# Attention feeding two expert layers on one core: a weight split spread over eight periods, and the order of the value products

## The chip, the core and the metric

One NeuronCore of a Trainium2 chip runs the whole kernel in one launch. The time is the device time of one execution in microseconds (us). The engines have short names in the profile: PE (TensorE matmul), PEld (its weight loads), DVE (VectorE), ACT (ScalarE), POOL (GpSimd) and SP (SyncE, which here only issues transfers). Each engine runs its own instructions in order and waits on the others through semaphores.

## The reference

What is computed, cut to what matters:

```python
# q, k, v: (2, 12, 448, 64) f32; cap = 30
scores = cap * tanh((q @ k.T / 8) / cap)
attn = softmax(scores) with 1e-9 added to the sum
x = (attn @ v) as (896, 768)
h = max(x @ w1, x @ w2, x @ w3); x = h @ w_out
xn = x / rms(x) * g
out = (silu(xn @ w_gate) * (xn @ w_val)) @ w_out2
```

The weights arrive in float64. A weight is used as a high and a low part, and so is each activation, so that a matrix product costs three matmuls.

## The kernel before, in words

**Attention.** The 24 heads are taken as 12 pairs; a pair's two heads lie on the two halves of the partitions. The 448 keys of a pair are four blocks: three of 128 (c = 0, 1, 2) and a last one of 64 (c = 3, `KB`), whose two heads share one tile. `scores(i, c)` multiplies keys by queries into PSUM banks (line 210 for the blocks of 128, line 217 for the last), and ACT takes tanh from each bank into the tile of exponents (lines 212, 218). There are five such banks, so a product waits for the tanh of the fifth before it. `expo(i)` (line 222) is two ACT instructions that take exp of blocks 0 and 1, then of 2 and 3. The sums over keys are built block on block: `sum_01` (line 226) and `sum_3` (line 231, two instructions, one for each head) on POOL, `sum_2` (line 235) on DVE; `sum_all` (line 253) is a product with ones that adds over the partitions. `values` (line 247) accumulates exponents times values over the four blocks in one bank. `norm` (lines 257, 259: a reciprocal and a product) and `split_x` (lines 267, 268) on DVE finish a pair and cut it into its high and low parts.

A function `period(i)` writes out by hand what each engine does: for period i, norm of pair i - 2, `sum_2` of pair i - 1, `split_x` of pair i - 2, then scores of pair i, values and `sum_all` of pair i - 1, exp and block sums of pair i. Period 12 (`period(n)`) runs in `tail`, a hook inside the first matrix product of the second stage. The fp32 products come in pairs of records, one pair for the two heads side by side, so a block of 128 keys is four records.

**Weights.** They come in units of 128 x 768 float64. `load_unit` (lines 98, 99) makes two transfers on SP, `raw` and `mid`, each with two buffers. `split_unit` (lines 109 to 117) turns a unit into `whi` and `wlo` by eight instructions, then calls `load_next`, which starts the next load. For the first two units all eight run on DVE (`on_dve`). Unit 0 is split in period 0, unit 1 in period 1, unit 2 in the tail, the others by a planner that spreads them over the matrix products.

**Start.** Two products of zeros (`warm`, line 316) run on PE before the first scores. In the bounded case, which these inputs take, the order is that of `period`.

**After the attention** the matrix products follow (lines 277 and 531), about 447 us of the span.

Of the kernel before, what the change touches and what calls it, by code (L numbers as in the profile page):

```python
# [18 lines left out]
B, H, S, D = 2, 12, 448, 64  # L19
# [3 lines left out]
NC = S // CP  # L23
KB = S // P
# [16 lines left out]
def attn_moe_kernel(ctx, tc, bounded, qT, kT, v, cap, w123, wo, wgv, wo2, rms_g, out):  # L41
    nc = tc.nc
    pe, dve, act, pool, sp = nc.tensor, nc.vector, nc.scalar, nc.gpsimd, nc.sync
# [31 lines left out]
    def bank():  # L75
        return pp.tile([P, 512], F32, tag="b", name="bank", bufs=5)

    def bank_o():
        return pp.tile([P, 512], F32, tag="o", name="banko", bufs=2)

    def bank_s():
        return pp.tile([P, 512], F32, tag="s", name="banks", bufs=1)
# [16 lines left out]
        sp.dma_start(out=mid.rearrange("p a b -> p (a b)").bitcast(U16)[:, :4 * U - 2], in_=src.bitcast(U16)[:, 1:4 * U - 1])  # L99
        return raw[:, :, 1], mid[:, :, 0]  # L100

    def split_unit(words, on_dve):
        hi, lo = (gp.tile([P, U], F32R, tag="g", name=name, bufs=NG) for name in ("whi", "wlo"))
        f = wp.tile([P, U], U32, tag="f", name="f", bufs=2)
        d = wp.tile([P, U], U32, tag="d", name="d", bufs=1)
        high, mid = words
        ff = f.bitcast(F32)
        steps = [
            (lambda: dve.tensor_scalar(f, high, 0x7FFFFFFF, None, op0=ALU.bitwise_and)) if on_dve else
            (lambda: act.activation(ff, high.bitcast(F32), AF.Abs)),  # L110
            lambda: dve.tensor_scalar(ff, ff, W_MIN, W_MAX, op0=ALU.max, op1=ALU.min),  # L111
            lambda: dve.tensor_scalar(f, f, 3, 0x3FFFF000, op0=ALU.logical_shift_left, op1=ALU.bitwise_and),
            lambda: dve.scalar_tensor_tensor(f, high, 0xC0000000, f, op0=ALU.bitwise_and, op1=ALU.bitwise_or),  # L113
            lambda: (dve.tensor_copy if on_dve else act.copy)(hi, ff),  # L114
            lambda: dve.tensor_scalar(d, f, 0xFF800000, None, op0=ALU.bitwise_and),  # L115
            lambda: dve.tensor_scalar(mid, mid, 0x01FFFFFF, None, op0=ALU.bitwise_and),
            lambda: dve.scalar_tensor_tensor(lo, mid, 2.0 ** -36, d.bitcast(F32), op0=ALU.mult, op1=ALU.mult),  # L117
            load_next,
        ]
        for step in steps:  # L120
            step()
        return hi, lo

    unit_src = [w123[j, n] for j in range(KC) for n in range(3)]
# [4 lines left out]
    loaded, units = [], []  # L129
# [2 lines left out]
        if len(loaded) < len(unit_src):  # L132
            loaded.append(load_unit(unit_src[len(loaded)]))

    def split_next():
        i = len(units)
        units.append(split_unit(loaded[i], i < 2))
        loaded[i] = None

    with tc.manual_schedule():  # L140

        pairs = [(b, hp) for b in range(B) for hp in range(NP)]
        n = len(pairs)
        kq, vt, E, EX, Ssum, SB, PO, XS = {}, {}, {}, {}, {}, {}, {}, {}
        X = [None] * KC

        def load_pair(i):

            b, hp = pairs[i]
            k_, qv = tp.tile([P, S], F32, tag="k", name="k", bufs=3), big("qv")  # L150
            kq[i], vt[i] = (k_, qv[:, 0]), qv[:, 1]
            sp.dma_start(out=k_, in_=kT[b, hp])
            sp.dma_start(out=qv[:, 0], in_=qT[b, hp])

        def load_v(i):
            b, hp = pairs[i]
            sp.dma_start(out=vt[i], in_=v[b, hp])
# [36 lines left out]
        def blocks(i):  # L194

            t = quad("e01"), quad("e23")
            E[i] = [t[0][:, 0], t[0][:, 1], t[1][:, 0], t[1][:, 1, 0]]
            EX[i] = t[0].rearrange("p a j s -> p (a j s)"), t[1].rearrange("p a j s -> p (a j s)")[:, :3 * S]

        def scores(i, c):  # L200
            if i not in E:
                blocks(i)
            t = E[i][c]
            k_, q_ = kq[i]
            heads = [slice(j * D, (j + 1) * D) for j in range(2)]
            if c < KB:

                ps = [bank(), bank()]
                for j, rows in enumerate(heads):
                    pe.matmul(ps[j][:, :S], k_[rows, c * P:(c + 1) * P], q_[rows], start=True, stop=True)  # L210
                for j in range(2):
                    act.activation(t[:, j, :], ps[j][:, :S], AF.Tanh, scale=tsc)  # L212
            else:

                ps = bank()
                for rows in heads:
                    pe.matmul(ps[rows, :S], k_[rows, KB * P:], q_[rows], start=True, stop=True)  # L217
                act.activation(t, ps[:, :S], AF.Tanh, scale=tsc)

        def expo(i):  # L220
            for e in EX[i]:
                act.activation(e, e, AF.Exp, scale=cap_sb)  # L222
# [5 lines left out]
        def sum_3(i, eng):  # L228
            for j in range(2):
                rows = slice(j * KL, (j + 1) * KL)  # L230
                eng.tensor_add(Ssum[i][rows, j], Ssum[i][rows, j], E[i][KB][rows])

        def sum_2(i):

            dve.scalar_tensor_tensor(Ssum[i], E[i][2], guard, Ssum[i], op0=ALU.add, op1=ALU.add)  # L235

        def values(i, *blocks):
            for c in blocks:
                if c == 0:
                    PO[i] = bank_o()  # L240
                for j in range(2):
                    if c < KB:
                        w, e = vt[i][:, c * P + j * D:c * P + (j + 1) * D], E[i][c][:, j, :]
                    else:
                        rows = slice(j * KL, (j + 1) * KL)
                        w, e = vt[i][rows, KB * P:], E[i][c][rows]
                    pe.matmul(PO[i][64 * j:64 * j + 64, :S], w, e, start=(c == 0), stop=(c == KB))  # L247

        def sum_all(i):

            ps = SB[i] = bank_s()
            for j in range(2):
                pe.matmul(ps[64 * j:64 * j + 64, :S], ones, Ssum[i][:, j, :], start=True, stop=True)  # L253

        def norm(i):
            r = small("r")[:, :S]
            dve.reciprocal(r, SB.pop(i)[:, :S])  # L257
            xs = XS[i] = spare()
            dve.tensor_mul(xs, PO.pop(i)[:, :S], r)

        def split_x(i):
            b, hp = pairs[i]
            if b == 0:
                X[hp] = flat("x")
            hi, lo = (t[:, BATCH[b]] for t in X[hp])
            xs = XS.pop(i)
            dve.tensor_copy(hi, xs)
            dve.tensor_sub(lo, xs, hi.bitcast(F32))
# [43 lines left out]
        dve.memset(warm, 0.0)  # L312
        act.activation(tsc, warm[:, :1], AF.Exp)
        ps = bank()
        for _ in range(2):
            pe.matmul(ps[:, :S], warm[:, :P], warm, start=True, stop=True)
        load_next()
        load_pair(1)
# [12 lines left out]
        if bounded:  # L331

            guard = const.tile([P, 1], F32, name="guard")
            dve.tensor_scalar_mul(guard, cap_sb, -1.0)
            dve.tensor_tensor(guard, guard, cap_sb, op=ALU.min)
            act.activation(guard, guard, AF.Exp)
            dve.tensor_scalar_mul(guard, guard, 1e-9 / P)
            def period(i):

                if i + 2 < n:
                    load_pair(i + 2)
                    load_v(i + 2)
                if i >= 2:
                    norm(i - 2)
                if i == n:
                    sum_3(i - 1, dve)
                if i >= 1:
                    sum_2(i - 1)  # L350
                if i == 1:
                    split_next()
                if i >= 2:
                    split_x(i - 2)
                if i < n:
                    for c in range(NC):
                        scores(i, c)
                if i >= 1:
                    values(i - 1, 0, 1, 2)
                    sum_all(i - 1)  # L360
                    values(i - 1, 3)
                if i < n:
                    expo(i)
                    if i == 0:

                        split_next()
                        sum_01(i, dve)
                        sum_3(i, dve)
                    else:
                        sum_01(i, dve if i == n - 1 else pool)  # L370
                        if i < n - 1:
                            sum_3(i, pool)

            def tail():
                period(n)
                split_next()
                norm(n - 1)
                split_x(n - 1)

            for i in range(n):  # L380
                period(i)
        else:
            for i in range(n):
                if i + 2 < n:
                    load_pair(i + 2)
                    load_v(i + 2)
                attend(i)
            for _ in range(3):
                split_next()
# [153 lines left out]
        first = {}  # L543
# [5 lines left out]
        for u in range(len(unit_src) - 1, 2, -1):  # L549
            e = min(first[u] - AHEAD, nxt - SPACE)  # L550
# [56 lines left out]
```

## Time and profile before

| what | us |
|---|---|
| three timed runs | 554.73, 554.96, 556.86 |
| median of them | 554.96 |
| the profiled execution, its own time | 556.08 |
| its span, first to last instruction | 554.3 |
| PE busy in it | 539.7 (97%) |
| DVE busy | 415.0 (75%) |
| ACT busy | 240.6 (43%) |
| POOL busy | 59.2 (11%) |

A row of the time line tells the start, the duration, the engine, the line and operation, the tile written and the tiles read, and how many records were merged; in brackets stands the idle time of the engine ahead of it and what ended it. The busy shares are means over the span: the attention is its first fifth, and the rest is matrix products. The granted clock is a share of TensorE's full rate, so 0.50 is 1.2 GHz and 1.00 is 2.4 GHz.

### The profile page before, as it was taken

How to read it: one execution, taken by the hardware profiler on the slowest of the kernel's cores; microseconds unless marked ns; L12 is line 12 of the kernel's file. 1: busy time of each engine (PE TensorE's matmuls, PEld its weight loads, DVE VectorE, ACT ScalarE, POOL GpSimd, SP SyncE). 2: the span in 40 equal slices, each digit the busy share in tenths (PEclk: the TensorE clock that was granted, in tenths of full speed). 3: DMA queues.
4: the chain of work that ended last, by engine and by line, in shares of the span. 5: the costliest groups of instructions: out<-in, count | busy, mean ns of one | idle time of the engine just before them, and what ended most of it. 6: DMA issues, size and time to landing. Idle time of an engine off the chain costs nothing.

```text
span 554.3 us, 7037 instructions
## 1 busy us (share of the span) xinstructions
PE 539.7 (97%) x2682; PEld 438.3 (79%) x2682; DVE 415.0 (75%) x592; ACT 240.6 (43%) x347; POOL 59.2 (11%) x48
## 2 busy tenths in 40 slices
PE   7879999999999999999999999999999999999996
PEld 3223333479889999988998999988888999999996
DVE  4996777799998898686586888878777778836701
ACT  4858898714434333335454333333333333312201
POOL 0335556300000000002122000000000000000000
PEclk9889999999999999999999999999999999999999
DMA  7843320037897878566500476666666666874402
GB/s 256 340 157 100 101 94 6 1 115 246 319 316 287 294 246 278 197 247 229 187 0 1 139 264 245 217 215 207 210 218 223 223 219 217 318 275 173 156 1 105
DMA packets 24810, 105.90 MB, mean 191 GB/s; under 512 B 3008, under 2 KB 9408, under 8 KB 24768
## 3 DMA queue, kind: packets, MB, share of 16 engines
q1 hardware_dynamic: 23760, 104.19, 54.0%
q10 hardware_dynamic: 1008, 1.18, 0.6%
q8 instruction: 23, 0.38, 0.3%
q14 instruction: 19, 0.16, 0.1%
HBM read 102.60 MB, written 2.75 MB: 190 GB/s over the span
## 4 chain that ended last, share of the span: by engine, by line
PE 96%; ACT 1%; DMA 1%; DVE 1%; SPq 0%; issue 0%
PE bank L277 40%; PE banko L277 16%; PE bank L531 10%; PE banko L247 8%; PE banks L277 7%; PE bank L210 6%; PE banko L531 3%; PE banks L531 2%; PE bank L217 2%; PE banks L253 2%; DMA qv<-in_qT 1%; DVE sum L235 1%; ACT e L222 1%; ACT e L212 0%; SPq L600 0%
## 5 line engine op out<-in xcount | busy, mean ns | idle before, releaser
L114 ACT CAST whi<-f 128x768 fp32r<-128x768 f32 x58 | 48.8, 841 | 150.7 <-DVE f L113 127.9
L277 PE MATMUL bank<-xn,whi 128*128 128x512 f32 (+1 forms) x360 | 102.9, 367 | 0.0
L277 PE MATMUL bank<-x,whi 128*128 128x512 f32 (+2 forms) x276 | 79.2, 368 | 0.0
L277 PEld LDWEIGHTS bank<-xn,whi 128*128 128x128 f32 x360 | 66.5, 188 | 8.2
L277 PE MATMUL bank<-xn,wlo 128*128 128x512 f32 (+1 forms) x180 | 66.2, 368 | 0.0
L117 DVE SCALAR_TENSOR_TENSOR wlo<-mid,d 128x768 fp32r<-128x768 uint32 x60 | 58.3, 972 | 5.1 <-PE banks L277 1.6
L113 DVE SCALAR_TENSOR_TENSOR f<-raw,f 128x768 uint32<-128x768 uint32 x60 | 57.5, 959 | 2.1
L277 PEld LDWEIGHTS bank<-x,whi 128*128 128x128 f32 x276 | 51.0, 188 | 7.4 <-issue 1.4
L531 PE MATMUL bank<-whi,a 128*128 128x384 f32 x216 | 54.8, 334 | 0.0
L110 ACT ACTIVATE f<-raw 128x768 f32<-128x768 f32 x58 | 52.6, 907 | 3.5 <-DMA raw<-in_wo 2.5
L277 PE MATMUL bank<-x,wlo 128*128 128x512 f32 (+2 forms) x138 | 50.8, 368 | 0.0
L111 DVE TENSOR_SCALAR f<-f 128x768 f32<-128x768 f32 x60 | 34.8, 581 | 17.4 <-ACT f L110 16.3
L212 ACT ACTIVATE e<-bank,tsc 128x448 f32<-128x448 f32 x72 | 39.3, 642 | 18.8 <-PE bank L210 12.0
L257 DVE RECIPROCAL r<-banks 128x448 f32<-128x448 f32 x12 | 35.5, 2955 | 11.3 <-PE banks L253 11.3
L247 PE MATMUL banko<-e,qv 128*64 128x448 f32 (+1 forms) x192 | 43.2, 572 | 0.0
L277 PE MATMUL banko<-xn,whi 128*128 128x512 f32 (+1 forms) x144 | 40.7, 364 | 0.0
L210 PE MATMUL bank<-qv,k 64*128 64x448 f32 x144 | 37.1, 607 | 2.5 <-ACT e L212 1.9
L531 PEld LDWEIGHTS bank<-whi,a 128*128 128x128 f32 x216 | 39.0, 188 | 0.0
L222 ACT ACTIVATE e<-e,cap_sb 128x1792 f32<-128x1792 f32 (+1 forms) x24 | 37.5, 1633 | 0.0
L115 DVE TENSOR_SCALAR d<-f 128x768 uint32<-128x768 uint32 x60 | 35.5, 592 | 2.0
L277 PEld LDWEIGHTS bank<-xn,wlo 128*128 128x128 f32 x180 | 33.8, 188 | 4.0
L531 PE MATMUL bank<-wlo,a 128*128 128x384 f32 x108 | 36.1, 334 | 0.0
(130 smaller groups left out, 877.7 us busy)
## 6 DMA issues: line engine op xcount, KB each, us to landing
raw<-in_wgv SPq DMA_DIRECT2D x24, 768.0 KB, 4.2
mid<-in_wgv SPq DMA_DIRECT2D x24, 767.5 KB, 5.3
raw<-in_w SPq DMA_DIRECT2D x18, 768.0 KB, 5.2
raw<-in_wo SPq DMA_DIRECT2D x18, 768.0 KB, 4.2
mid<-in_w SPq DMA_DIRECT2D x18, 767.5 KB, 5.6
mid<-in_wo SPq DMA_DIRECT2D x18, 767.5 KB, 5.4
k<-in_kT SPq DMA_DIRECT2D x12, 224.0 KB, 3.1
qv<-in_qT SPq DMA_DIRECT2D x12, 224.0 KB, 3.5
```

The source lines that it names most:

```text
L110: (lambda: act.activation(ff, high.bitcast(F32), AF.Abs)),
L113: lambda: dve.scalar_tensor_tensor(f, high, 0xC0000000, f, op0=ALU.bitwise_and, op1=ALU.bitwise_or),
L114: lambda: (dve.tensor_copy if on_dve else act.copy)(hi, ff),
L115: lambda: dve.tensor_scalar(d, f, 0xFF800000, None, op0=ALU.bitwise_and),
L117: lambda: dve.scalar_tensor_tensor(lo, mid, 2.0 ** -36, d.bitcast(F32), op0=ALU.mult, op1=ALU.mult),
L210: pe.matmul(ps[j][:, :S], k_[rows, c * P:(c + 1) * P], q_[rows], start=True, stop=True)
L212: act.activation(t[:, j, :], ps[j][:, :S], AF.Tanh, scale=tsc)
L222: act.activation(e, e, AF.Exp, scale=cap_sb)
L247: pe.matmul(PO[i][64 * j:64 * j + 64, :S], w, e, start=(c == 0), stop=(c == KB))
L257: dve.reciprocal(r, SB.pop(i)[:, :S])
L277: pe.matmul(ps, a[:, k, :], x[k][h][:, cols], start=(k == 0 and n_ == 0), stop=(k == KC - 1 and n_ == 2))
L531: pe.matmul(acc_o[s][:, :HN], a[:, ts], w[:, sl], start=(k == 0 and n_ == 0), stop=(k == FC - 1 and n_ == 2))
```

## The change

- `split_unit` may put its nine steps (eight DVE instructions and `load_next`) into a list instead of running them. Unit 1 is no longer split at once in period 1: from period 2 on, behind `split_x`, each period runs one step, and period 9 runs the last two, so that unit 3's load is issued there.
- In period 1 the values of pair 0 are put between the scores of pair 1: blocks 0 and 1 behind the scores' first two blocks, blocks 3 and 2 behind the others, then `sum_all(0)`.
- In all other periods the values come in the order 3, 0, 1, 2, and `sum_all` comes last; before, it stood between blocks 2 and 3.
- `values` finds its first and last block by counting, not by the block's number.
- A third product of zeros runs at the start.

```diff
--- before.py
+++ after.py
@@ -99,7 +99,7 @@
         sp.dma_start(out=mid.rearrange("p a b -> p (a b)").bitcast(U16)[:, :4 * U - 2], in_=src.bitcast(U16)[:, 1:4 * U - 1])
         return raw[:, :, 1], mid[:, :, 0]
 
-    def split_unit(words, on_dve):
+    def split_unit(words, on_dve, defer=None):
         hi, lo = (gp.tile([P, U], F32R, tag="g", name=name, bufs=NG) for name in ("whi", "wlo"))
         f = wp.tile([P, U], U32, tag="f", name="f", bufs=2)
         d = wp.tile([P, U], U32, tag="d", name="d", bufs=1)
@@ -117,8 +117,11 @@
             lambda: dve.scalar_tensor_tensor(lo, mid, 2.0 ** -36, d.bitcast(F32), op0=ALU.mult, op1=ALU.mult),
             load_next,
         ]
-        for step in steps:
-            step()
+        if defer is None:
+            for step in steps:
+                step()
+        else:
+            defer.extend(steps)
         return hi, lo
 
     unit_src = [w123[j, n] for j in range(KC) for n in range(3)]
@@ -132,16 +135,16 @@
         if len(loaded) < len(unit_src):
             loaded.append(load_unit(unit_src[len(loaded)]))
 
-    def split_next():
+    def split_next(defer=None):
         i = len(units)
-        units.append(split_unit(loaded[i], i < 2))
+        units.append(split_unit(loaded[i], i < 2, defer))
         loaded[i] = None
 
     with tc.manual_schedule():
 
         pairs = [(b, hp) for b in range(B) for hp in range(NP)]
         n = len(pairs)
-        kq, vt, E, EX, Ssum, SB, PO, XS = {}, {}, {}, {}, {}, {}, {}, {}
+        kq, vt, E, EX, Ssum, SB, PO, XS, done = {}, {}, {}, {}, {}, {}, {}, {}, {}
         X = [None] * KC
 
         def load_pair(i):
@@ -236,15 +239,17 @@
 
         def values(i, *blocks):
             for c in blocks:
-                if c == 0:
+                first = i not in PO
+                if first:
                     PO[i] = bank_o()
+                done[i] = done.get(i, 0) + 1
                 for j in range(2):
                     if c < KB:
                         w, e = vt[i][:, c * P + j * D:c * P + (j + 1) * D], E[i][c][:, j, :]
                     else:
                         rows = slice(j * KL, (j + 1) * KL)
                         w, e = vt[i][rows, KB * P:], E[i][c][rows]
-                    pe.matmul(PO[i][64 * j:64 * j + 64, :S], w, e, start=(c == 0), stop=(c == KB))
+                    pe.matmul(PO[i][64 * j:64 * j + 64, :S], w, e, start=first, stop=(done[i] == NC))
 
         def sum_all(i):
 
@@ -312,7 +317,7 @@
         dve.memset(warm, 0.0)
         act.activation(tsc, warm[:, :1], AF.Exp)
         ps = bank()
-        for _ in range(2):
+        for _ in range(3):
             pe.matmul(ps[:, :S], warm[:, :P], warm, start=True, stop=True)
         load_next()
         load_pair(1)
@@ -335,6 +340,8 @@
             dve.tensor_tensor(guard, guard, cap_sb, op=ALU.min)
             act.activation(guard, guard, AF.Exp)
             dve.tensor_scalar_mul(guard, guard, 1e-9 / P)
+            steps = []
+
             def period(i):
 
 
@@ -348,17 +355,29 @@
                     sum_3(i - 1, dve)
                 if i >= 1:
                     sum_2(i - 1)
-                if i == 1:
-                    split_next()
                 if i >= 2:
                     split_x(i - 2)
-                if i < n:
-                    for c in range(NC):
-                        scores(i, c)
-                if i >= 1:
-                    values(i - 1, 0, 1, 2)
-                    sum_all(i - 1)
-                    values(i - 1, 3)
+
+                    if i == 2:
+                        split_next(steps)
+                    for step in steps[:1 if i < 9 else None]:
+                        step()
+                    del steps[:1 if i < 9 else None]
+                if i == 1:
+                    scores(1, 0)
+                    scores(1, 1)
+                    values(0, 0, 1)
+                    scores(1, 2)
+                    scores(1, 3)
+                    values(0, 3, 2)
+                    sum_all(0)
+                else:
+                    if i < n:
+                        for c in range(NC):
+                            scores(i, c)
+                    if i >= 1:
+                        values(i - 1, 3, 0, 1, 2)
+                        sum_all(i - 1)
                 if i < n:
                     expo(i)
                     if i == 0:
```

## Rows read from the trace of the kernel before

**Rows 1.** What PE waited for, over the whole span (us in total, times, longest).
```profile
PE banks L253 <- DVE sum L235: 3.8, 1, 3.8
PE bank L316 <- DVE warm L312: 3.2, 1, 3.2
PE bank L210 <- ACT e L212: 1.9, 1, 1.9
PE bank L210 <- DMA qv<-in_qT: 0.6, 1, 0.6
```

**Rows 2.** Chain of work, 0 to 110 us: start, us, engine, tile, line, count.
```profile
7.12 4.68 PE bank L210 x12
...
31.25 3.00 DVE sum L235
...
35.36 1.69 PE banko L247 x4
37.05 3.53 PE bank L210 x12
...
45.53 2.75 PE bank L210 x12
48.27 0.90 PE bank L217 x4
...
51.58 0.75 PE banks L253 x4
52.33 0.90 PE banko L247 x4
...
107.14 3.03 PE bank L277 x14
```

**Rows 3.** PE by windows of 2 us: length, busy, granted clock, DMA share, GB/s.
```profile
36.00:38.00 2.00, 2.00 (x8) 0.50 0.00 0
```

**Rows 4.** Time line of the start, 0 to 22 us.
```profile
3.16 3.33 PE L316 MATMUL bank<-warm 128*128 128x448 f32 x4 [3.16 <-DVE warm L312]
...
10.56 0.56 DVE L112 TENSOR_SCALAR f<-f 128x768 uint32<-128x768 uint32 x1
...
11.16 0.96 DVE L113 SCALAR_TENSOR_TENSOR f<-raw,f 128x768 uint32<-128x768 uint32 x1
...
13.34 3.10 ACT L222 ACTIVATE e<-e,cap_sb 128x1792 f32<-128x1792 f32 x2
...
16.32 3.26 ACT L212 ACTIVATE e<-bank,tsc 128x448 f32<-128x448 f32 x6
...
20.06 3.09 ACT L222 ACTIVATE e<-e,cap_sb 128x1792 f32<-128x1792 f32 x2
```

**Rows 5.** Time line of periods 1 and 2, 21.5 to 48 us.
```profile
22.07 2.45 DVE L115 TENSOR_SCALAR d<-f 128x768 uint32<-128x768 uint32 x1
...
31.22 2.07 POOL L226 TENSOR_TENSOR sum<-e 128x896 f32<-128x896 f32 x1 [4.29 <-ACT e L222]
31.25 2.98 DVE L235 SCALAR_TENSOR_TENSOR sum<-e,guard,sum 128x896 f32<-128x896 f32 x1
```

**Rows 6.** Time line of period 4, 44 to 62 us.
```profile
46.57 3.25 ACT L212 ACTIVATE e<-bank,tsc 128x448 f32<-128x448 f32 x6 [0.94 <-POOL sum L226]
46.63 2.32 POOL L231 TENSOR_TENSOR sum<-sum,e 64x448 f32<-64x448 f32 x2
...
48.98 1.15 DVE L235 SCALAR_TENSOR_TENSOR sum<-e,guard,sum 128x896 f32<-128x896 f32 x1 [0.59 <-POOL sum L231]
...
50.20 3.13 ACT L222 ACTIVATE e<-e,cap_sb 128x1792 f32<-128x1792 f32 x2
50.47 0.63 DVE L268 TENSOR_TENSOR x<-xs,x 128x448 fp32r<-128x448 f32 x1
...
52.17 2.08 POOL L226 TENSOR_TENSOR sum<-e 128x896 f32<-128x896 f32 x1 [3.22 <-ACT e L222]
...
52.41 2.96 DVE L257 RECIPROCAL r<-banks 128x448 f32<-128x448 f32 x1 [1.31 <-PE banks L253]
```

## The prediction

> **What bounds the kernel now.** I read the waits of PE first. PE has four waits in the whole span, 9.5 us together, and all lie in the attention [rows 1]; the matrix products behind it never wait, so a microsecond taken out of the attention is a microsecond of the kernel. Then the chain of waits up to 110 us [rows 2]: it is PE nearly throughout, with one piece of DVE, 31.25 to 34.25, where PE waits 3.8 us for `sum_2` of pair 1. Behind that wait PE runs at half clock: the windows grant 0.50, which is 1.2 GHz, after that standstill [rows 3]; the values' last block takes 1.69 instead of 0.90 and the scores 3.53 instead of 2.75 [rows 2]. From 45.53 to 107.14 eight periods pass unbroken, 61.61 / 8 = 7.70 each. The slack is therefore ahead of 45.53, and the DVE row says why: `sum_2` is queued behind unit 1's split, whose instruction of 0.56 us [rows 4] takes 2.45 while POOL adds [rows 5].
>
> **The change part by part.** All times are of the profiled execution, 556.08.
>
> *Warm-up.* Two products take four records and 3.33 us cold, from 3.16 [rows 4]; their pace is about 0.75, which is what the 12 cold score records also give for a pair (4.68 / 6 = 0.78, against 2.75 / 6 = 0.46 warm [rows 2]). A third adds 2 x 0.75 = 1.5 us. PE stood idle for 0.6 ahead of the first scores at 7.12 [rows 1, 2], so these move back by 1.5 - 0.6 = 0.9, to 8.0. Whether the clock then rises sooner the trace can't show. It was low through the first scores and high for the second pair's. Without the idle gap it may rise near 8 us; at worst it rises where it did. Bounds for the first exp, T, which was 13.34 [rows 4]: late, 13.34 + 0.9 = 14.2; early, scores at 8.0, the first tanh 46.57 - 45.53 = 1.04 behind them [rows 2, 6], seven tanhs in 50.20 - 46.57 = 3.63 [rows 6], so 12.7.
>
> *Start of the attention, with the split gone from period 1.* ACT is now the chain. From exp to exp of two pairs it takes 20.06 - 13.34 = 6.7, and exp to next tanh 2.98 [rows 4]. Exp 1 starts at T + 6.7, the first tanh of pair 2 at T + 9.7. PE's part fits under it: values 0 and 1 of pair 0 run while ACT does the second exp, where PE waited 1.9 for a bank [rows 1], the others behind pair 1's scores. The two extra switches of tile shape that this mixing makes cost what a switch costs elsewhere, 0.90 - 0.75 = 0.15 each [rows 2], and lie in that idle time: nothing; without the cover 0.3. Pair 1's last scores wait for the bank of its second tanh, T + 2.98 + 2 x 0.54 = T + 4.1 (3.26 / 6 [rows 4]); with them, values 3 and 2 and `sum_all(0)`, 4 x 0.75, and some 0.8 for switches and the bank, `sum_all(0)` ends about T + 7.9, so the reciprocal (2.96 [rows 6]) of pair 0 is done by T + 11.1, before POOL has the sums of pair 1 ready, at exp 1 + 1.97 + 2.08 + 2.32 + 0.1 = T + 13.2 (the offset is 52.17 - 50.20, the durations [rows 6]). The last block of scores(2) comes 1.7 after its first tanh (48.27 against 46.57 [rows 2, 6]), at T + 11.4; the rest of a period, below, is 7.54 - 2.75 = 4.8 long, so scores(3) start at T + 16.2: 28.9 early, 30.4 late. Before they started at 37.05.
>
> *Order 3, 0, 1, 2.* The last block's values (64 x 64 tiles) cost 0.90 where four records without a switch cost 0.75, as `sum_all` behind values of the same shape [rows 2]. Now they follow the last scores, which have this shape too: one switch less, 0.15 to 0.16 a period, 7.54 instead of 7.70. Against this stands a rule of the Trainium skill, page "TensorE: Matmul & The Clock Gate", section "The mechanism": a weight load overlaps running matmuls only where the row groups differ. By it the loads of block 3 would wait just as now and the saving would be nothing; the row of `sum_all`, whose loads take the same 128 rows as the values in front, shows no gap. I take the row, and the rule is a rival.
>
> *The split's steps.* Six instructions of about 0.56 and two of 0.96 [rows 4], 5.3 us, go to periods 2 to 9. DVE had 1.31 idle per period [rows 6], and PE's new order puts `sum_all` 0.75 later, so its reciprocal too; `sum_2` still ends over 1 us before `sum_all` needs it, since this now comes at 6.8 of a period. One step fits. `load_next` moves with them: unit 3's two transfers leave SP's queue ahead of pair 4's loads and stand behind pair 11's, where SP waits for the last step and nothing else is queued until the tail. Unit 3 is split in the matrix products, tens of us later. In the tail `sum_all(11)` ends one block later, 0.9; its readers stand behind unit 2's split on DVE and under two matrix products: nothing, and at most 0.9 without them.
>
> *Sum.* Before: 37.05 + 8.48 + 8 x 7.70 = 107.1 [rows 2]. After: 28.9 to 30.4, and nine periods of 7.54, 67.9: 96.8 to 98.3. The gain is 8.8 to 10.3; I take the middle, 9.6, as no row decides the clock. 556.08 - 9.6 = 546.5. The median of the timed runs is 1.1 below the profiled execution; I leave that to the range.
>
> **The rivals.**
>
> *B, one collision.* A step that meets POOL waits. In period 2 `sum_2` starts at T + 13.2, and cast and difference end 51.10 - 48.98 = 2.12 later [rows 6], at T + 15.3; the step starts there. POOL's next add starts at exp 2 + 1.97 = T + 13.4 + 2.0 = T + 15.4 [rows 4, 6]. That is a tie. If POOL is first, the step waits some 1.9 (2.45 - 0.56 [rows 4, 5]), the reciprocal is 1.5 late, in period 3 the difference falls under POOL's add too (2.98 for 1.15 shows the size [rows 5]), and `sum_2` of pair 3 makes PE wait about 3, with half clock behind it, 0.79 + 0.78 and some [rows 2]: 5 us given back once, then DVE has caught up. 546.5 + 5 = 551.5. For it: the tie. Against: in later periods POOL starts 7.54 + 1.97 behind the last exp, 0.9 behind the step's place.
>
> *E, no switch is saved (the rule above):* block 3's loads wait as in the rows of before, 9 x 0.16 = 1.4 less gain, 547.9.
>
> *D, the collision comes twice,* as DVE does not catch up: 546.5 + 10 = 556.5, no change.
>
> *C, slower: DVE's queue becomes the period.* DVE's own work is 2.96 for the reciprocal, 0.63 for the product (taken as long as the difference), 2.12 from `sum_2` to the difference's end and 0.56 for a step, 6.3 [rows 4, 6]. If in each period with a step three of its four lockable instructions wait out an add, 3 x 1.2 (half of 2.32 [rows 6]), it is 9.9, 2.4 over PE's 7.54; over seven periods 16.8, against the 9.6 gained: 563. It decides against the change from 7.54 + 9.6 / 7 = 8.9 a period on. For it: each late piece of DVE falls deeper under POOL. Against: the early wait of PE lets DVE catch up, as it did at 36 us.
>
> *F, the third product only delays:* that is the late end of T and lies in the forecast.
>
> **How the numbers follow.** Forecast 0.45, own range 544 to 548 (T early with the median's 1.1 off, and T late); E 0.10; B 0.27; something between B and D that still gains, 0.05; D 0.06; C 0.07. Faster by over 0.5% (2.8 us, about what a measurement of this kernel tells from no change): 0.45 + 0.10 + 0.27 + 0.05 = 0.87; same 0.06; slower 0.07. The range 544.0 to 552.0 takes in the forecast, E and B.
>
> **What would show it.** Right: PE's wait for `sum_2` is gone, the scores of pair 3 start near 29, periods last 7.54, the exp of pair 0 starts at 12.7 or 14.2, and the values' first block stands 0.37 behind the last scores without a gap. B: a step of period 2 or 3 with 2 us or more, and a PE wait for `sum_2` near 43. C: that wait in most periods. E: periods of 7.70. The forecast is wrong if PE still waits for DVE after 30 us, or if a wait shows up behind 100 us.

## The result and the profile after

The changed kernel takes 545.52 us (median of 6 runs, 544.38 to 547.0) against 554.85 for the kernel before (6 runs, 552.04 to 556.86); the ratio is 0.9842, 95% interval 0.981 to 0.9875. The forecast was 546.5, between 544 and 552. The profiled execution took 545.16, its span is 543.4: 10.9 below that of before. The forecast was worked out for the profiled execution, so 545.16 is what it has to be held against first.

PE's waits over the whole span, of the changed kernel, stand against [rows 1]:

```profile
PE bank L321 <- DVE warm L317: 3.2, 1, 3.2
PE bank L213 <- ACT e L221: 1.2, 1, 1.2
```

In this execution the waits for `sum_2` and for the first queries are gone; what is left besides the start is one wait of 1.2 in period 1. The line numbers moved: 213 and 220 are the scores, 215 and 221 their tanh, 225 the exp, 229 and 234 POOL's sums, 238 `sum_2`, 252 the values, 258 `sum_all`, 262 the reciprocal, 272 and 273 `split_x`, 282 the first matrix products, 321 the products of zeros; the split keeps 109 to 117.

The chain of waits of the changed kernel, against [rows 2]:

```profile
3.15 4.49 PE bank L321 x6
...
7.64 1.04 PE bank L213 x4
...
28.49 2.69 PE bank L213 x12
...
32.07 3.16 PE banko L252 x16
35.23 0.75 PE banks L258 x4
35.98 2.75 PE bank L213 x12
...
96.42 3.84 PE bank L282 x18
```

Before, scores(3) started at 37.05 and the matrix products at 107.14; now it is 28.49 and 96.42. From 35.98 on there are eight periods, (96.42 - 35.98) / 8 = 7.55 each, against 7.70. Values and `sum_all` need 3.16 + 0.75 = 3.91 instead of 2.41 + 0.75 + 0.90 = 4.06. The twelve score records of pair 0 now take 2.73, from PE's time line; before, they took 4.68.

```profile
7.64 2.73 PE L213 MATMUL bank<-qv,k 64*128 64x448 f32 x12
```

That is 0.23 a record, as in the later periods (2.75 for twelve at a granted 1.00, 2.4 GHz), where it was 0.39. From 8 to 10 us the windows grant 1.00 in both kernels, so for this stretch the durations tell the two paces apart and that column doesn't.

DVE and POOL in period 2 of the changed kernel, where the prediction saw a tie; first the time line of DVE:

```profile
25.39 1.15 DVE L238 SCALAR_TENSOR_TENSOR sum<-e,guard,sum 128x896 f32<-128x896 f32 x1 [1.37 <-POOL sum L234]
...
26.88 0.63 DVE L273 TENSOR_TENSOR x<-xs,x 128x448 fp32r<-128x448 f32 x1
27.42 0.56 DVE L109 TENSOR_SCALAR f<-raw 128x768 uint32<-128x768 uint32 x1
28.56 2.96 DVE L262 RECIPROCAL r<-banks 128x448 f32<-128x448 f32 x1 [0.57 <-PE banks L258]
```

The time line of POOL in the same kernel:

```profile
27.58 2.35 POOL L229 TENSOR_TENSOR sum<-e 128x896 f32<-128x896 f32 x1 [2.22 <-ACT e L225]
```

The split's step starts at 27.42, POOL's add at 27.58. The step came first by 0.16 us, and the add, 2.08 elsewhere [rows 6], took 2.35. It is no toss of a coin from run to run: in the nine profiles with this meeting, of this kernel and its variants, the lead is 0.16 or 0.17 each time, though the first exp came anywhere from 12.16 to 13.96.

### The profile page after: what moved, and what is told of

The parts are those of the page before. It is cut to its first block, busy times and chain, and to the rows that moved or that the text cites. A ratio compares the mean times of both kernels' runs of the same rounds, so it can differ in the third digit from the quotient of the medians.

```text
span 543.4 us, 7028 instructions
## 1 busy us (share of the span) xinstructions
PE 534.0 (98%) x2684; PEld 438.4 (81%) x2684; DVE 407.0 (75%) x592; ACT 240.1 (44%) x347; POOL 58.3 (11%) x48
## 3 DMA queue, kind: packets, MB, share of 16 engines
HBM read 102.60 MB, written 2.75 MB: 194 GB/s over the span
## 4 chain that ended last, share of the span: by engine, by line
PE 98%; ACT 1%; DVEq 0%; DVE 0%; issue 0%
PE bank L282 41%; PE banko L282 16%; PE bank L550 10%; PE banks L282 7%; PE banko L252 7%; PE bank L213 6%; PE banko L550 3%; PE banks L550 2%; PE bank L220 2%; PE banks L258 2%; PE bank L321 1%; ACT e L215 0%; DVEq L619 0%; PE bank L452 0%; ACT e L221 0%
## 5 line engine op out<-in xcount | busy, mean ns | idle before, releaser
L252 PE MATMUL banko<-e,qv 128*64 128x448 f32 (+1 forms) x192 | 40.2, 546 | 0.0
L213 PE MATMUL bank<-qv,k 64*128 64x448 f32 x144 | 34.4, 562 | 1.2 <-ACT e L221 1.2
L112 DVE TENSOR_SCALAR f<-f 128x768 uint32<-128x768 uint32 x60 | 33.6, 560 | 2.0
```

The lines of the kernel that those rows point to most:

```text
L252: pe.matmul(PO[i][64 * j:64 * j + 64, :S], w, e, start=first, stop=(done[i] == NC))
```

## The experiments

Ten variants and two repeats, each beside runs of the kernel before on the same chip. Diffs show only what differs, `...` stands between places that lie apart, and all are against the changed kernel, except the second.

**The split back in period 1.**

```diff
+                if i == 1:
+                    split_next()
...
-                    if i == 2:
-                        split_next(steps)
-                    for step in steps[:1 if i < 9 else None]:
-                        step()
-                    del steps[:1 if i < 9 else None]
```

> The changed kernel with one part undone: unit 1 is split at once in period 1 again; third warm-up product, mixed period 1 and order 3, 0, 1, 2 stay. Theory (the moved split carries most of the gain): sum_2 of pair 1 is late behind the split, PE waits for it 2 to 4 us in period 2 and runs at half clock after it, so 5 to 8 of the 9 to 11 us are lost: 551 to 553. Rival (the gain is that of the warm-up and of PE's order, and the split only fills a gap): the time stays within 2 us of the changed kernel, 545 to 547.

552.74 us (551.71 to 554.53), ratio to before 0.996, 0.9931 to 0.999. PE's waits:

```profile
PE banks L258 <- DVE sum L238: 4.2, 1, 4.2
```

Its chain in period 2:

```profile
27.41 2.88 DVE r L262
...
30.85 1.60 DVE sum L238
...
32.59 1.76 PE banks L258 x4
34.35 3.51 PE bank L213 x12
```

The window behind the stall (length, busy, granted clock, DMA share, GB/s):

```profile
34.00:36.00 2.00, 2.00 (x8) 0.51 0.43 161
```

The old stall is back behind the split, and half clock (0.51, so 1.2 GHz) behind the stall: 1.76 for 0.75, 3.51 for 2.75. Of the 9.3 us, 552.74 - 545.52 = 7.2 hang on the split by the medians, 6.5 by the two ratios.

**The split alone, on the kernel before.** Its edit is the deferred steps (and the counting in `values`, which changes nothing in the old order).

```diff
+                    if i == 2:
+                        split_next(steps)
+                    for step in steps[:1 if i < 9 else None]:
+                        step()
+                    del steps[:1 if i < 9 else None]
-                if i == 1:
-                    split_next()
```

> The kernel before with one part done: unit 1's split one step a period; two warm-up products, old order of the values, period 1 not mixed. Theory: the wait of 3.8 for sum_2 and the half clock behind it go, 5 to 7 us: 548 to 550; period 1 keeps its wait of 1.9 for a bank, and periods last 7.70. Rival (the parts need each other: without PE's later sum_all the steps make DVE late): PE still waits for sum_2 in some period and the gain is under 3 us.

550.49 (548.23 to 552.29), ratio 0.9913, 0.9892 to 0.9934: by the ratio 4.8 us gained. The profiled execution was the fastest of the four. In it PE doesn't wait for `sum_2` in any period; its waits are 1.3 for the first queries and 1.2 and 1.0 for ACT, and periods last 7.70. So the steps don't need the other parts, and the split is worth 4.8 alone and 6.5 to 7.2 beside them.

**Two warm-up products, twice.**

```diff
-        for _ in range(3):
+        for _ in range(2):
```

> The changed kernel with two warm-up products in place of three. Theory: the first scores start at about 7.1 again, but run at 1.2 GHz up to 10 or 11 us, and the first exp comes between 0.2 earlier and 1.0 later than with three; the time is 0 to 1.5 us longer: 545.5 to 547. Rival (the third product is only a delay): 0.5 to 0.9 shorter.

546.53 (544.61 to 547.14), ratio 0.9826, 0.9806 to 0.9846. That can't be told from the changed kernel's 0.9842. In this profile the first scores ran fast (2.73), but PE then stood still for 1.6 us until the queries of pair 1 had landed, and the clock fell; PE by windows of 2 us (length, busy, granted clock, DMA share, GB/s):

```profile
12.00:14.00 2.00, 1.27 (x4) 0.76 1.08 446
14.00:16.00 2.00, 2.00 (x8) 0.50 0.97 401
```

So both were run once more on one chip, the changed kernel itself and the one with two products.

> The changed kernel itself once more, so that it stands on the same chip beside its variants: 544 to 547, periods of 7.55. A run with a wait for sum_2 among them would show that the near meeting in period 2 goes the other way at times.

> The changed kernel with two warm-up products once more, beside the changed kernel on the same chip. Theory: 0.5 to 1.5 us longer than it, as the clock rises later or falls again. Rival: no difference that these runs can tell, as the first exps hang on the transfer of the first queries and on ACT.

The changed kernel took 545.32 (544.39 to 545.62), with two products 546.70 (546.40 to 547.34). The runs don't overlap: 1.4 us for the third product on this chip. The chain with two products shows the slow scores of before, 4.87 for twelve records; the time line has the exp of pair 0 at 13.96, against 12.50 in the changed kernel's profile of this pair of runs:

```profile
7.54 4.87 PE bank L213 x12
```

```profile
13.96 3.10 ACT L225 ACTIVATE e<-e,cap_sb 128x1792 f32<-128x1792 f32 x2
```

The two attentions end at 98.04 and 96.62, so the 1.4 is the later exp. But two products don't always start slowly. Of four profiles with two of them, two have slow first scores, behind an idle PE of 0.6 and 0.9 us (4.64 and 4.84 for twelve), and two have fast ones, behind 1.1 and 1.3 us (2.73 each). In the eight profiles with three products and the scores of pair 0 in this order they take 2.73 to 3.39. So what three products bring is that the fast start comes every time; that they do it by filling PE's gap isn't shown.

No run of the changed kernel, twelve in all, was above 547.0, so the near meeting of period 2 went the same way in each, as far as times can tell; in its two profiles the step led by 0.16 and 0.17 (27.61 against 27.78 in the repeat).

**The old order of the values.**

```diff
-                        values(i - 1, 3, 0, 1, 2)
-                        sum_all(i - 1)
+                        values(i - 1, 0, 1, 2)
+                        sum_all(i - 1)
+                        values(i - 1, 3)
```

> The changed kernel with the values in the old order (0, 1, 2, sum_all, 3) in all periods but the first. Theory (one switch of tile shape less a period): periods last 7.70 in place of 7.55 and nine of them cost 1.4 us: about 547. Rival E (weight loads can't be drawn ahead within a row group, so that nothing was saved by it): periods and time as in the changed kernel. A third way: sum_all comes 0.75 earlier, sum_2 isn't ready, and PE waits for DVE: over 2 us.

547.67 (546.83 to 547.88), ratio 0.9853, 0.9837 to 0.9869; the intervals overlap, so the times alone don't decide. The chain does:

```profile
43.97 2.75 PE bank L213 x12
...
51.67 2.75 PE bank L213 x12
```

A period is 51.67 - 43.97 = 7.70, and PE has no wait for DVE. Against 7.55 it is 0.15 over nine periods, 1.4 us. Up to scores(3) the two profiles are 0.13 apart (28.62 and 28.49), at the end of the attention 1.46 (97.88 and 96.42). Rival E is out. In the changed kernel the weight loads show why (time line of PEld):

```profile
38.66 0.19 PEld L220 LDWEIGHTS bank<-qv,k 64*64 64x64 f32 x4 [0.65 <-ACT e L215]
39.09 0.14 PEld L252 LDWEIGHTS banko<-e,qv 64*64 64x64 f32 x2 [0.24 <-issue]
39.46 0.14 PEld L252 LDWEIGHTS banko<-e,qv 64*64 64x64 f32 x2 [0.24 <-issue]
40.31 0.20 PEld L252 LDWEIGHTS banko<-e,qv 128*64 128x64 f32 x4 [0.70 <-issue]
```

The loads for block 3 follow those of the last scores at PE's pace of 0.37 while the scores' matmuls run, in the same row groups; those of the next shape come 0.70 idle later. The Trainium skill's rule (page "TensorE: Matmul & The Clock Gate", section "The mechanism"), that a load overlaps running matmuls only where the row groups differ, doesn't hold for these rows; the same section also names loads drawn ahead into a background weight buffer, which would fit them. In these rows the idle stretches of 0.65 and 0.70 stand where the tile shape changes, and 0.24 where it doesn't.

**Period 1 not mixed.**

```diff
-                if i == 1:
-                    scores(1, 0)
...
-                    sum_all(0)
-                else:
```

> The changed kernel with period 1 not mixed: all of pair 1's scores, then pair 0's values 3, 0, 1, 2 and its sums. Theory (ACT sets the pace up to the third pair, so PE's idle time there is worth little): PE waits some 2 us for a bank in period 1 again, the third pair's scores come later by that less what ACT's pace hides, 0.5 to 1.5 us: 546 to 547. Rival (PE's wait counts in full): 2 us or more, above all if the clock falls behind the wait.

546.66 (545.76 to 548.85), ratio 0.9861, 0.9826 to 0.9897: some 1.2 above the changed kernel, which these intervals don't separate. In its profile scores(3) start at 30.13, 1.6 later than 28.49. But that can't be put on the order of period 1: PE stood still for the queries of pair 1, a transfer, until 13.37, where the changed kernel began these scores at 12.50, and the granted clock was 0.54 from 14 to 16 us, behind a stretch where PE was busy 0.63 of 2 us. The row of PE's time line, then two windows:

```profile
13.37 4.45 PE L213 MATMUL bank<-qv,k 64*128 64x448 f32 x12 [2.03 <-DMA qv<-in_qT]
```

```profile
12.00:14.00 2.00, 0.63 (x4) 1.00 1.06 435
14.00:16.00 2.00, 2.00 (x8) 0.54 1.02 426
```

**The first step twice in period 2.** This asks what the tie was worth.

```diff
                     if i == 2:
                         split_next(steps)
+                        steps[0]()
```

> The changed kernel with the first step of the split run twice in period 2 (0.56 us more on DVE, the same values). In the changed kernel this step starts 0.16 ahead of POOL's add. Theory (rival B of the prediction: what comes behind the start of POOL's add waits it out): the second one waits some 2 us, the reciprocal of pair 1 is 1.5 late, PE waits about 3 for sum_2 in period 3 or 4, then half clock: 3 to 6 us longer, 549 to 551. Rival (DVE's spare time takes it up): no PE wait, and less than 0.5 longer.

556.78 (551.18 to 558.4, 12 runs), ratio 1.0019, 0.9984 to 1.0053: all of the gain is lost to one instruction of 0.56 us. Nine runs lie between 556.53 and 558.40, three between 551.18 and 551.42. PE's waits in its profiled execution:

```profile
PE banks L258 <- DVE sum L238: 8.3, 4, 3.4
```

DVE's time line:

```profile
27.89 2.91 DVE L109 TENSOR_SCALAR f<-raw 128x768 uint32<-128x768 uint32 x2
30.73 2.94 DVE L262 RECIPROCAL r<-banks 128x448 f32<-128x448 f32 x1
...
35.73 2.40 DVE L273 TENSOR_TENSOR x<-xs,x 128x448 fp32r<-128x448 f32 x1
...
44.03 2.27 DVE L272 CAST x<-xs 128x448 fp32r<-128x448 f32 x1
...
52.63 2.28 DVE L238 SCALAR_TENSOR_TENSOR sum<-e,guard,sum 128x896 f32<-128x896 f32 x1
...
63.95 2.45 DVE L114 CAST whi<-f 128x768 fp32r<-128x768 f32 x1
```

POOL's time line:

```profile
28.05 2.34 POOL L229 TENSOR_TENSOR sum<-e 128x896 f32<-128x896 f32 x1 [2.23 <-ACT e L225]
...
35.55 2.10 POOL L229 TENSOR_TENSOR sum<-e 128x896 f32<-128x896 f32 x1 [2.57 <-ACT e L225]
...
63.80 2.19 POOL L229 TENSOR_TENSOR sum<-e 128x896 f32<-128x896 f32 x1 [6.66 <-issue]
```

The second copy starts at 28.48, behind the add of 28.05, and waits it out. The reciprocal starts at 30.73, in the changed kernel at 28.56. From then on another instruction falls under each add, always an earlier one of the queue: the difference at 35.73, the cast at 44.03, `sum_2` itself at 52.63. PE waits for `sum_2` twice in this. That lets DVE catch up, but at 63.95 the step of period 6 starts 0.15 behind an add, and a second cascade runs to the end of the attention, with two more waits. The first cascade cost PE 4.0 us of waiting, the second 4.4. That the three times near 551 are runs with one cascade is a guess; none of them was profiled.

**The step of period 6 twice.** The same 0.56 us, in a period where there is room ahead of the add.

```diff
+                    if i == 6:
+                        steps[0]()
                     for step in steps[:1 if i < 9 else None]:
```

> The changed kernel with the step of period 6 run twice (0.56 us more on DVE, the same values), as the step of period 2 was in the run of the doubled step. In period 6 the step ends 0.4 ahead of POOL's add, in period 2 its end falls behind the add's start. Theory (it is the meeting with POOL's add that costs, not the 0.56): the second one starts ahead of the add, POOL gives way by 0.2, no PE wait, within 0.5 us of the changed kernel. Rival (DVE has no room for 0.56 more in any period): the cascade of waits for sum_2, 5 to 11 us longer.

545.88 (544.46 to 546.83), ratio 0.9838, 0.9807 to 0.987: no difference. DVE's time line:

```profile
57.03 1.15 DVE L114 CAST whi<-f 128x768 fp32r<-128x768 f32 x2
59.03 2.96 DVE L262 RECIPROCAL r<-banks 128x448 f32<-128x448 f32 x1 [0.85 <-PE banks L258]
```

POOL's time line:

```profile
58.04 2.08 POOL L229 TENSOR_TENSOR sum<-e 128x896 f32<-128x896 f32 x1 [3.07 <-issue]
```

The two copies lie between 57.03 and 58.18, both started ahead of the add, and DVE is idle 0.85 behind them. So it is not the 0.56 that costs 11 us, but where it falls.

**All eight steps in period 2.**

```diff
                     if i == 2:
-                        split_next(steps)
-                    for step in steps[:1 if i < 9 else None]:
-                        step()
-                    del steps[:1 if i < 9 else None]
+                        split_next()
```

> The changed kernel with all eight steps at once in period 2, in the place where its first step stands. Theory (spreading is what counts): 5.3 us of DVE work, with waits for POOL up to 9, stand ahead of pair 1's reciprocal and of sum_2 of pair 2; PE waits 4 to 6 us for it in period 3, half clock follows: 551 to 553. Rival (being past period 1 is what counts): within 1.5 us of the changed kernel.

555.94 (555.01 to 557.1), ratio 1.0021, 0.9998 to 1.0044. PE waits 7.5 us for `sum_2`, once. The expectation named the right side with too small a number: the eight steps, 5.3 us of work, lie from 28.37 to 38.93 on DVE, since four of them meet POOL; DVE's time line:

```profile
28.97 2.32 DVE L111 TENSOR_SCALAR f<-f 128x768 f32<-128x768 f32 x1
31.32 1.37 DVE L112 TENSOR_SCALAR f<-f 128x768 uint32<-128x768 uint32 x1
32.73 1.77 DVE L113 SCALAR_TENSOR_TENSOR f<-raw,f 128x768 uint32<-128x768 uint32 x1
...
36.09 2.84 DVE L117 SCALAR_TENSOR_TENSOR wlo<-mid,d 128x768 fp32r<-128x768 uint32 x1
```

Moving the whole split from period 1 to period 2 is worth nothing; spreading it is what pays.

**Two other orders on PE.** Twelve score records take 2.75 in each period, where twelve at the pace of `sum_all` (0.75 for four) would take 2.25. I put most of the difference down to a wait for a bank, though PE's list of waits has none in these periods; both runs tried to save it.

```diff
+                    if i >= 2:
+                        values(i - 1, 3)
-                        for c in range(NC):
+                        for c in (3, 0, 1, 2):
-                        values(i - 1, 3, 0, 1, 2)
+                        values(i - 1, 0, 1, 2)
```

> The changed kernel with another order on PE in the periods from 2 on: values 3 of the pair before, then the scores in the order 3, 0, 1, 2, then values 0, 1, 2 and the sums (period 0 takes its scores in that order too). In the profile the third block of scores waits for a bank in each period, and the rows of a block without that wait give 0.6 to 0.7 us a period. Theory: the one-bank block first spares that wait, the number of switches stays, periods last 6.9 to 7.1 as ACT takes at least 6.6: 4 to 6 us shorter, 540 to 542. Rival (DVE and POOL, which have 6.3 us of work and a lock between them, can't follow at 7): PE waits for sum_2, and the time is that of the changed kernel or longer.

560.46 (559.76 to 560.82), ratio 1.0103, 1.007 to 1.0137. Neither theory came true: PE waits for ACT's exp 11 times (15.1 us). The values of block 3, ahead of the scores, need the exp of the pair before, which ends only there, and the scores behind them hold up ACT in turn. My expectation had overlooked that dependency.

```diff
-                        for c in range(NC):
+                        for c in (3, 0, 1, 2):
```

> The changed kernel with the scores in the order 3, 0, 1, 2 in all periods but the second; the values stay behind the scores, so that they don't wait for the exp of the pair before as in the run of the other order. Theory (the third block's wait for a bank, 0.6 to 0.7 a period, goes; one switch of tile shape more, 0.15 to 0.25): periods of 7.1 to 7.3, ten of them 3 to 4 us shorter: 541 to 543. Rival: ACT, which then gets one bank, pauses, and gets the next, or DVE under POOL's lock can't keep 7.2: periods of 7.55 or more, 545 or longer.

546.77 (546.15 to 547.54), ratio 0.9852, 0.9822 to 0.9882. Periods are 7.64, from this chain:

```profile
37.18 0.90 PE bank L220 x4
38.08 2.69 PE bank L213 x12
40.76 3.31 PE banko L252 x16
...
44.82 0.90 PE bank L220 x4
```

The twelve records take 2.69 still, so nothing of the difference was saved, and the values take 3.31 for 3.16, one switch more. Neither version beats the changed kernel.

## Why the prediction was right

**The stall and the split.** As predicted: the wait for `sum_2` and the half clock behind it were DVE's queue, and the steps fit one to a period. Put back, the split costs 6.5 to 7.2; alone it brings 4.8.

**The start.** T, the exp of pair 0, came at 12.30, 0.4 ahead of the early bound; scores(3) at 28.49 against 28.9 to 30.4. From T to scores(3) the prediction had 16.2, and 16.19 came, so the whole miss lies ahead of T. The term that was mis-sized is the warm-up: 3.33 + 1.5 = 4.8 us and scores at 8.0 were expected, but it took 4.49 for six records, the scores started at 7.64, and they ran at full pace at once. From there the early bound holds: 7.64 + 1.04 + 3.63 = 12.31. The size isn't fixed, though: in the repeat the six records took 4.74 and T was 12.50, and in six variants they took 4.82. The attention ended 1.1 sooner than the middle of 96.8 and 98.3: 0.75 of that is the middle taken between early and late, 0.4 the scores' earlier start. So the gain in the attention, 107.14 - 96.42 = 10.7, lies above the 8.8 to 10.3 that were worked out. ACT as the chain is seen in the exps of the changed kernel:

```profile
12.30 3.13 ACT L225 ACTIVATE e<-e,cap_sb 128x1792 f32<-128x1792 f32 x2
...
18.91 3.18 ACT L225 ACTIVATE e<-e,cap_sb 128x1792 f32<-128x1792 f32 x2
...
25.51 3.23 ACT L225 ACTIVATE e<-e,cap_sb 128x1792 f32<-128x1792 f32 x2
```

They are 6.6 apart, where 6.7 was taken.

**The third product** was no delay (F): 1.4 us on one chip. With two of them PE ran the first scores slowly in two profiles of four (4.64 and 4.84 for twelve records); with three they took 3.39 at most.

**The order 3, 0, 1, 2** gave 7.55 for the 7.54 forecast; the row of `sum_all` decided rightly against the Trainium skill's rule, and E is out.

**The mixing of period 1** was argued to be covered. The 1.2 us between the medians aren't separated from nothing, and the profile can't decide, since in it the queries of pair 1 came later and the clock fell. What the mixing is worth stays open.

**The rivals.** B named the right place and the right mechanism, and the tie was real: 0.16 us decided it. The rows could not tell which way it would fall, so that the forecast escaped B was luck, though it fell this way in every profile. Its size was wrong in the main. I wrote that 5 us would be given back once, "then DVE has caught up". With the meeting forced by one more instruction, three runs of twelve lost some 6 us, as B has it (551.2 to 551.4 against 551.5), and nine lost 11, which is D's 556.5, to which I gave 0.06. In the profile of such a run DVE did catch up, as B says, but then a later step starts a second cascade. C didn't occur: in periods 3 to 6 of the changed kernel the step starts 0.7 to 1.0 ahead of the add (34.40 against 35.08 in period 3, 41.62 against 42.63 in period 4).

**The sum.** 7.2 for the split, 1.4 for the order, 1.4 for the third product and about 1.2 for the mixing make 11.2, against 9.3 between the medians and 10.9 between the two profiled executions. Each is good to about 1 us, and the last isn't told from nothing, so this is agreement and no more. That the forecast gain of 9.6 lies so near the 9.3 is in part chance: it was a gain between profiled executions, and there 10.9 came. The profiled execution of before was 1.2 above its median and that of the changed kernel 0.4 below, which is the difference between the two gains.

**Unit 3's load and the tail** cost nothing: PE has no wait behind 100 us.

## What to carry to other kernels

Where two engines exclude each other, the cost of a small instruction is not its duration but whether it starts ahead of the other engine's long one; look up both start times, and give such a step a period with room. Work that is not due soon is worth spreading over the idle time of a queue, one piece a period, more than it is worth moving as a whole. Products of one tile shape belong next to each other, here 0.15 us a switch.

## What was not expected of the hardware

One more instruction of 0.56 us, started 0.4 us behind an add of POOL, cost 11 us in nine runs of twelve, as each DVE instruction that waited out an add of POOL (2.27 to 2.45 in the rows above, for 0.39 to 1.15) pushed an earlier one of the next period under the next add. The rule that fits is in the Trainium skill, page "SBUF — State Buffer", section "SBUF: two separate sides": GpSimd, and DVE in a two-port mode or with two inputs in SBUF, hold the ports that they share for a whole instruction, and whoever starts first keeps them. The rows agree: the step that started 0.16 ahead of the add made it 2.35 long, and the second copy, which started 0.43 behind one, ended only after it.
